# A quarter of the MLP's inner rows for chunks 0 to 8, worked out in native fp32 products while the attention runs

## The chip, the cores and the metric

The kernel runs on one core of one Trainium2 chip. The metric is the device time of one execution in microseconds (us); smaller is better. In every trace TensorE is PE (its weight loads PEld), VectorE is DVE, ScalarE is ACT, GpSimd is POOL and SyncE is SP.

## The reference

Two stages, in fp32. A recurrent attention over 768 steps for 4 batches and 8 heads of width 40, and then an MLP on its output for 3072 tokens:

```python
for t in range(S):                                  # attention: r, k, v, w, a, b are (4, 8, 768, 40)
    y[:, :, t] = np.einsum('bhd,bhde->bhe', rt, state)
    Sa = np.einsum('bhde,bhe->bhd', state, at)
    state_decay = state * wt[:, :, None, :] - np.einsum('bhd,bhe->bhde', Sa, bt)
    state = state_decay + np.einsum('bhd,bhe->bhde', vt, kt)
x = y.transpose(0, 2, 1, 3).reshape(3072, 320)
h = x @ w_in                                        # w_in is (320, 2048)
sp = np.where(h > 20.0, h, np.log1p(np.exp(np.minimum(h, 20.0))))
out = (h * np.tanh(sp)) @ w_out                     # Mish; w_out is (2048, 320)
```

## The kernel before

The 768 steps are cut into 12 chunks of 64; a chunk holds 256 tokens of the MLP. The attention has three kinds of work. `pre_a` (four times for two chunks) loads wa and bk through SP, makes running products of the decay on DVE, writes them to memory as pD, and multiplies on PE into `pa` tiles (L186, L202). `pre_inv` and `post_inv` invert a triangular matrix for two chunks, first on DVE (L214, L216), then on PE, and make the KT tiles (L258). `step` is the recurrence itself, one chunk after another: L284 into `pu`, negated by ACT into UVT (L286), transposes (L293, L304), L314 into `pq`, masked by DVE into UVQ (L316), then L334 and L339, from which DVE takes the new state and ACT the output yev, which goes to memory as yD through POOL's queue. All products of the attention are native fp32.

The MLP reads yD and pD of a chunk back (`load_x`, eight DMAs on SP), multiplies them on DVE (L565), and splits the result into a high and a low part of type fp32r (xh, xl). Each weight is split in the same way (`split`: a DMA of 512 or 640 columns into cv_d, ACT, three DVE instructions, ACT, DVE). The 2048 inner rows are worked through in four quarters q of 512. For a quarter, `mlp1` makes 32 products of 256 columns into `ph` (L583), ACT applies Mish (L585) and rounds (L588), DVE takes the low part (L589); `mlp2` makes 24 products of 320 columns into `po` (L603 to L605), three quarters later. After the fourth quarter ACT copies po out (L609) and SP stores it.

The pieces of weights are converted in stages that the program names: `early` (the first quarter of w_in: three pieces, at the start of the attention), `first` (the other three quarters: nine pieces, after the last `pre_a`), `second` (w_out pieces 0 to 2, behind the last `post_inv`) and `third` (w_out 3 to 7). The number of cv_d buffers of a stage is CVE, CVA, CVD, CVC. PSUM has eight banks: two for pu, two for pq, two for the pa of the inverse (`ps_a`), two for the pa of `pre_a` (`ps_g`); in the MLP four of them are ph and four po.

The framework sorts each engine's instructions into one list when the program is built, by priorities, by when it expects operands and buffers to be there, and by its own estimates of cost; OFF holds offsets of priority for parts of the program (positive is earlier). The engine then works through its list from front to back.

Of the kernel before, what the change touches and what calls it, by code (L numbers as in the profile page):

```python
# [7 lines left out]
F32 = mybir.dt.float32  # L8
# [8 lines left out]
NBKN = 8  # L17
NA = 2
NWA = 2
# [5 lines left out]
NGP = 2  # L25
NG = 2
NQ = 2
# [9 lines left out]

OFF = {'I': 80, 'T1': 80, 'P00': -40, 'P10': 80, 'P11': 40, 'b0': 15, 'c0': 600, 'u0': -15, 'u1': 250, 'd0': 250,
       'd1': 150, 'W': 600, 'V': 400, 'E': 150, 'I0': 600, 'I1': -15, 'I2': 15, 'I3': 150, 'I4': 80, 'p4': 15,
# [39 lines left out]
def attention(ctx, tc, I, yD, pD, nch, M):  # L79
# [336 lines left out]
NQ0 = 1  # L416
NQ1 = 4
NO1 = 3
CVW = 512
CVO = 640  # L420
CVE = 1
CVD = 1
CVA = 1
CVB = 1
CVC = 2
NX = 2
NXP = 1
NHB = 3
# [16 lines left out]
def load_f32(nc, pool, w, src):  # L445

    V, A, SP = nc.vector, nc.scalar, nc.sync
    n = w.shape[1]
    if src.dtype == F32:
        SP.dma_start(out=w, in_=src)  # L450
        return 1.0
    d = pool.tile([128, n, 2], I32, name="cv_d")
    SP.dma_start(out=d.rearrange("p a b -> p (a b)"), in_=src.bitcast(I32))
    lo, hi = d[:, :, 0], d[:, :, 1]
    m = pool.tile([128, n], I32, name="cv_m")
    w = w.bitcast(I32)


    A.mul(m.bitcast(F32), hi.bitcast(F32), 2.0 ** -111)

    V.tensor_scalar(w, m, 0xfffffff, 3, op0=ALU.bitwise_and, op1=ALU.logical_shift_left)
    V.scalar_tensor_tensor(out=w, in0=m, scalar=-0x80000000, in1=w, op0=ALU.bitwise_and, op1=ALU.bitwise_or)
    V.scalar_tensor_tensor(out=w, in0=lo, scalar=29, in1=w, op0=ALU.logical_shift_right, op1=ALU.bitwise_or)
    return 2.0 ** -8
# [14 lines left out]
class Mlp:  # L479


    def __init__(self, ctx, tc, I, yD, pD, out):
        self.ctx, self.tc, self.I, self.yD, self.pD, self.out = ctx, tc, I, yD, pD, out
        self.ih, self.il, self.oh, self.ol = [], [], [], []

# [11 lines left out]
    def w_in(self, wp, cv, qs):  # L497
        for q in qs:
            h = wp.tile([128, 3, 512], F32R, name=f"w_ih{q}")
            l = wp.tile([128, 3, 512], F32R, name=f"w_il{q}")  # L500
            self.ih.append(h)
            self.il.append(l)
            for k in range(3):
                for c in range(0, 512, CVW):
                    s = slice(c, c + CVW)
                    self.split(cv, h[:, k, s], l[:, k, s], self.I['wi'][:, (q * 3 + k) * 512 + c:(q * 3 + k) * 512 + c + CVW])

    def w_out(self, wp, cv, qs):
        for q in qs:
            h = wp.tile([128, 640], F32R, name=f"w_oh{q}")  # L510
            l = wp.tile([128, 640], F32R, name=f"w_ol{q}")
            self.oh.append(h)
            self.ol.append(l)
            for c in range(0, 640, CVO):
# [3 lines left out]
    def early_pools(self, ctx):  # L518
        if NQ0:
            self.wpe = self.pool("w2e", 1)  # L520
            self.cve = ctx.enter_context(self.tc.tile_pool(name="cve", bufs=CVE, side="right"))

    def early(self):
        if NQ0:
            self.w_in(self.wpe, self.cve, range(NQ0))

    def first(self):
        wp = self.pool("w2a", 1)
        with self.tc.tile_pool(name="cva", bufs=CVA, side="right") as cv:
            self.w_in(wp, cv, range(NQ0, NQ1))  # L530

    def second(self):
        self.ps_h = self.pool("ps_h", NH, space=PSUM)
        if NQ1 < 4:
            wp = self.wp = self.pool("w2b", 1)
            with self.tc.tile_pool(name="cvb", bufs=CVB, side="right") as cv:
                self.w_in(wp, cv, range(NQ1, 4))
        self.mpx = self.pool("mpx", 2)
        self.mpa = self.pool("mpa", 2)
        if NO1:  # L540
            wp = self.pool("w2d", 1)
            with self.tc.tile_pool(name="cvd", bufs=CVD, side="right") as cv:
                self.w_out(wp, cv, range(NO1))

# [5 lines left out]
    def run(self, nsc):  # L550
# [7 lines left out]
        def load_x(i):  # L558
            y = self.mpx.tile([128, 3, T], F32, name="xy", bufs=NXP)
            p = self.mpx.tile([128, 3, T], F32, name="xp", bufs=NXP)  # L560
            load_yp(nc, i, yD, pD, y, p, True)
# [3 lines left out]
            V.tensor_tensor(out=y, in0=y, in1=p, op=ALU.mult)  # L565
# [3 lines left out]
            return xh, xl  # L569

        def mlp1(q, xh, xl):
            g = mpa.tile([128, 4, T], F32, name="g", bufs=NHB)
# [20 lines left out]

        def mlp2(i, q, gh, gl):
            if q == 0:
                pos[i] = [ps_o.tile([128, 320], F32, name="po") for _ in range(2)]
            po = pos[i]
            for j in range(4):
                f = q * 4 + j
                for k in range(2):  # L600
                    t = slice(k * 128, k * 128 + 128)
                    oh, ol = (w[f // 2][:, f % 2 * 320:f % 2 * 320 + 320] for w in (W.oh, W.ol))
                    PE.matmul(po[k], gh[:, j, t], oh, start=(f == 0), stop=False, skip_group_check=True)  # L603
                    PE.matmul(po[k], gh[:, j, t], ol, start=False, stop=False, skip_group_check=True)  # L604
                    PE.matmul(po[k], gl[:, j, t], oh, start=False, stop=(f == 15), skip_group_check=True)  # L605
            if q == 3:
                for k in range(2):
                    o = mp.tile([128, 320], F32, name="os")
                    A.copy(o, po[k])  # L609
                    SP.dma_start(out=out[i * T + k * 128:i * T + k * 128 + 128], in_=o)  # L610
# [3 lines left out]
        for i in range(nsc):  # L614
            for q in range(4):
                wait.append((i, q) + mlp1(q, *x))
                if (i, q) == (0, 0):
                    self.third()
                if q == 1 and i + 1 < nsc:
                    nx = load_x(i + 1)  # L620
# [7 lines left out]
def build(tc, I, out, nch):  # L628
    with ExitStack() as ctx:
        dp = ctx.enter_context(tc.tile_pool(name="dp", bufs=1, space=bass.MemoryType.DRAM))  # L630
        yD = dp.tile([nch, 2, 40, 2, 512], F32, name="yD")
        pD = dp.tile([nch, 2, 40, 2, 520], F32, name="pD")
        M = Mlp(ctx, tc, I, yD, pD, out)
        with ExitStack() as actx:
# [23 lines left out]
```

## Time and profile before

| | |
|---|---|
| median of three runs | 835.8 us (835.5 to 837.83) |
| span of the profiled execution | 843.5 us |
| mean granted PE clock | 0.939 |
| PE busy | 748.6 us (89%), 7816 records |
| PEld busy | 695.6 us (82%) |
| DVE busy | 462.0 us (55%) |
| ACT busy | 429.0 us (51%) |
| POOL busy | 103.3 us (12%) |

The span is from the first to the last instruction of one execution; no other time of that execution is listed, and it lies 7.7 us above the median of the runs. PE's busy time counts a record from its start to its modelled end, so records that follow closely overlap: where the prediction needs the cost of a product, it takes the distance between starts. A native fp32 product leaves two records in the trace, an fp32r product one.

```profile
PE   2645898998989889889799899999999999999998
DVE  6789879739899658788924639221222222122110
ACT  4533647774586866566738546333333333333331
PEclk9855689899999999899959999999999999999999
```

Each digit is the busy share of a fortieth of the span (21 us) in tenths. The attention fills the first 24 of them, the MLP the rest, where PE alone is full.

### The profile page before, as it was taken

The numbers are of one execution on the slowest core, as the hardware profiler recorded it, in microseconds if no ns is written. First come the engines' busy times: TensorE is split into PE (matmuls) and PEld (weight loads), VectorE is DVE, ScalarE is ACT, GpSimd is POOL, SyncE is SP. The second block draws the span as 40 slices with busy tenths as digits, with TensorE's granted clock in tenths as the row PEclk, the third lists the DMA queues.
The fourth block names the chain that finished last, engine by engine and source line by source line (L and its number), as shares of the span: only waits on it lengthen the run. The fifth ranks groups of instructions, "written<-read, shape, count | busy, mean of one in ns | idle before, by whom it ended". The sixth has DMA issues, their size and how long they took to land.

```text
span 843.5 us, 18796 instructions
## 1 busy us (share of the span) xinstructions
PE 748.6 (89%) x7816; PEld 695.6 (82%) x7816; DVE 462.0 (55%) x975; ACT 429.0 (51%) x937; POOL 103.3 (12%) x182
## 2 busy tenths in 40 slices
PE   2645898998989889889799899999999999999998
PEld 2534697887868778778768799999999999999998
DVE  6789879739899658788924639221222222122110
ACT  4533647774586866566738546333333333333331
POOL 8100012113122023221101200000000000000000
PEclk9855689899999999899959999999999999999999
DMA  6422223323423233323425734211120111100000
GB/s 177 134 71 64 74 63 73 90 67 105 129 81 80 66 88 103 82 67 96 123 66 142 179 109 128 54 35 36 38 54 25 31 54 35 35 21 16 16 1 32
DMA packets 58212, 61.91 MB, mean 73 GB/s; under 512 B 25536, under 2 KB 48704, under 8 KB 58128
## 3 DMA queue, kind: packets, MB, share of 16 engines
q1 hardware_dynamic: 49296, 40.94, 17.6%
q0 software_dynamic: 8832, 19.79, 9.5%
q8 instruction: 61, 1.00, 0.5%
q14 instruction: 23, 0.19, 0.1%
HBM read 48.79 MB, written 11.86 MB: 72 GB/s over the span
## 4 chain that ended last, share of the span: by engine, by line
PE 62%; DVE 15%; ACT 15%; issue 5%; DMA 2%; ACTq 0%; DVEq 0%; SPq 0%
PE ph L583 21%; PE po L604 7%; PE po L605 7%; PE po L603 7%; PE pa L186 5%; PE pa L258 4%; PE pq L314 3%; PE pq L334 2%; DVE XL L216 2%; DVE tmp L214 2%; ACT ad L155 2%; PE pu L284 1%; DMA cv_d<-in_wo 1%; DVE P L147 1%; ACT bdT L250 1%
## 5 line engine op out<-in xcount | busy, mean ns | idle before, releaser
L583 PE MATMUL ph<-xh,w_ih 128*128 128x256 f32 x576 | 148.3, 283 | 0.5 <-ACT xh L566 0.5
L585 ACT ACTIVATE g<-ph 128x512 f32<-128x512 f32 x96 | 57.3, 598 | 179.3 <-PE ph L583 179.2
L589 DVE TENSOR_TENSOR gl<-g,gh 128x1024 fp32r<-128x1024 f32 x48 | 58.7, 1225 | 160.7 <-ACT gh L588 160.4
L583 PE MATMUL ph<-xh,w_il 128*128 128x256 f32 x576 | 123.6, 283 | 0.0
L186 PE MATMUL pa<-bk,ad 128*128 128x168 f32 x384 | 85.0, 373 | 42.7 <-DVE bk L170 15.0
L604 PE MATMUL po<-w_ol,gh 128*128 128x320 f32 x384 | 118.8, 310 | 0.1
L605 PE MATMUL po<-w_oh,gl 128*128 128x320 f32 x384 | 118.4, 309 | 0.0
L603 PE MATMUL po<-w_oh,gh 128*128 128x320 f32 x384 | 117.7, 309 | 0.0
L186 PEld LDWEIGHTS pa<-bk,ad 128*128 128x128 f32 x384 | 70.8, 233 | 47.8 <-issue 22.8
L583 PEld LDWEIGHTS ph<-xh,w_ih 128*128 128x128 f32 x576 | 109.3, 190 | 0.7 <-ACT xh L566 0.7
L583 PE MATMUL ph<-xl,w_ih 128*128 128x256 f32 x384 | 101.2, 285 | 0.0
L583 PEld LDWEIGHTS ph<-xh,w_il 128*128 128x128 f32 x576 | 96.3, 190 | 0.0
L583 PEld LDWEIGHTS ph<-xl,w_ih 128*128 128x128 f32 x384 | 73.1, 190 | 0.8 <-issue 0.5
L604 PEld LDWEIGHTS po<-w_ol,gh 128*128 128x128 f32 x384 | 72.1, 188 | 0.5 <-DVE w_ol L495 0.5
L605 PEld LDWEIGHTS po<-w_oh,gl 128*128 128x128 f32 x384 | 72.1, 188 | 0.1
L603 PEld LDWEIGHTS po<-w_oh,gh 128*128 128x128 f32 x384 | 71.8, 188 | 0.0
L258 PE MATMUL pa<-bdT,HA 128*104 128x128 f32 x384 | 57.0, 304 | 9.0 <-ACT bdT L251 7.3
L258 PEld LDWEIGHTS pa<-bdT,HA 128*104 128x104 f32 x384 | 49.9, 190 | 14.4 <-ACT bdT L251 9.1
L216 DVE TENSOR_TENSOR XL<-XL,tmp 128x30 f32<-128x30 f32 (+9 forms) x180 | 59.0, 328 | 2.4
L214 DVE TENSOR_TENSOR tmp<-XL 128x30 f32<-128x30 f32 (+9 forms) x180 | 58.5, 325 | 2.5
L314 PE MATMUL pq<-bdr,UVT 128*128 128x128 f32 x384 | 57.3, 294 | 2.3 <-DVE UVQ L316 1.5
L314 PEld LDWEIGHTS pq<-bdr,UVT 128*128 128x128 f32 x384 | 50.8, 205 | 4.0 <-DVE UVQ L316 1.9
(89 smaller groups left out, 1243.5 us busy)
## 6 DMA issues: line engine op xcount, KB each, us to landing
wa<-in_wa SPq DMA_DIRECT2D x48, 162.5 KB
bk<-in_bk SPq DMA_DIRECT2D x48, 160.0 KB
cv_d<-in_wi SPq DMA_DIRECT2D x12, 512.0 KB
cv_d<-in_wo SPq DMA_DIRECT2D x8, 640.0 KB
pD<-P POOLq DMA_DIRECT2D x48, 81.2 KB, 2.2
VS<-in_vN POOLq DMA_DIRECT2D x24, 160.0 KB, 3.6
UVT<-in_vD POOLq DMA_DIRECT2D x24, 160.0 KB, 3.9
bdr<-in_rD POOLq DMA_DIRECT2D x24, 160.0 KB, 4.4
```

The costliest lines, as they stand in the source:

```text
L155: A.copy(ad[q, :, :, al], a[q].rearrange("p (s k t) -> p s k t", k=2, t=32))
L186: PE.matmul(pt[:, j], ad[:, s0 + j].rearrange("p k a t -> p (k a t)"), bk[:, s0 + j], start=(j == 0), stop=True, skip_group_check=True)
L214: V.tensor_tensor(out=tv, in0=X[:, i + 1:32, i:i + 1].broadcast_to([128, 31 - i, i]), in1=X[:, i:i + 1, 0:i].broadcast_to([128, 31 - i, i] ...
L216: V.tensor_tensor(out=X[:, i + 1:32, 0:i], in0=X[:, i + 1:32, 0:i], in1=tv, op=ALU.add)
L258: PE.matmul(pk[:, j], ha[:, s0 + j], bd[:, s0 + j].rearrange("p a t -> p (a t)"), start=(j == 0), stop=True, skip_group_check=True)
L314: PE.matmul(pq[:, s], UVT[:, g * 4 + s, be * 128:be * 128 + 128], br[:, be, g * 4 + s].rearrange("p a t -> p (a t)"), start=(s == 0), stop ...
L583: PE.matmul(o, w, x, start=(j == 0 and n == 0), stop=(n == 7), skip_group_check=True)
L585: A.activation(g[:, f0:f0 + 2], ph, AF.Mish)
L589: V.tensor_tensor(out=gl, in0=g, in1=gh.bitcast(F32), op=ALU.subtract)
L603: PE.matmul(po[k], gh[:, j, t], oh, start=(f == 0), stop=False, skip_group_check=True)
L604: PE.matmul(po[k], gh[:, j, t], ol, start=False, stop=False, skip_group_check=True)
L605: PE.matmul(po[k], gl[:, j, t], oh, start=False, stop=(f == 15), skip_group_check=True)
```

## The change

For chunks 0 to 8 the first quarter of the inner rows (q = 0) leaves the MLP. A new function `fill` does it: it loads y of a finished chunk, makes 12 native fp32 products of 256 columns with an unsplit copy of the first quarter of w_in (L541), Mish into gn, eight native products of 320 columns with the first quarter of w_out (L548), in two blocks of four, and stores the two partial results in memory (`part`, L560). It is written behind step i + 1 of the attention, with a priority that is 3000 lower; the load of y and its product (L530) keep the normal one. In the MLP the chunk then has three quarters, and DVE adds the partial result, read back through SP, where ACT copied. Chunks 9 to 11 do the same first quarter natively inside the MLP (`first_quarter` in `load_x`, `second_quarter` in `mlp2`), summed in po.

Buffers: the two pa pools become one of three banks (`ps_r`), and `fill` has one bank (`ps_f`). xy, xp and gn have one buffer each, shared by fills and MLP. The weights' stages change: `early` loads eight unsplit pieces (four of w_in with 384 columns, four of w_out with 320), `first` six pieces with two buffers, `second` three of w_in and three of w_out with one buffer, `third` three.

```diff
-NA = 2
-NG = 2
+NR = 3
+NF = 9
-OFF = {'I': 80, 'T1': 80, ...
+OFF = {'F': -3000, 'I': 80, 'T1': 80, ...
...
-    ps_a = pool("ps_a", NA, ictx, "right", space=PSUM)
+    ps_a = ps_g = pool("ps_r", NR, ictx, "right", space=PSUM)
+    ps_f = pool("ps_f", 1, ictx, "right", space=PSUM)
     M.early_pools(pctx)
-    ps_g = pool("ps_g", NG, pctx, "right", space=PSUM)
...
                 step(2 * n + int(k))
+                if 0 <= 2 * n + int(k) - 1 < NF:
+                    M.fill(2 * n + int(k) - 1, ps_f)
...
-NO1 = 3
+NO1 = 5
-CVA = 1
+CVA = 2
...
+    def load_y(self, i):
+        y = self.wpe.tile([128, 3, 256], F32, name="xy")
+        p = self.wpe.tile([128, 3, 256], F32, name="xp")
+        load_yp(self.tc.nc, i, self.yD, self.pD, y, p, True)
+        self.tc.nc.vector.tensor_tensor(out=y, in0=y, in1=p, op=ALU.mult)
+        return y
+
+    def first_quarter(self, y, ps):
+        nc = self.tc.nc
+        g = self.wpe.tile([128, 4, 256], F32, name="gn")
+        for f0 in (0, 2):
+            ph = ps.tile([128, 2, 256], F32, name="ph")
+            for j in range(2):
+                f = slice((f0 + j) * 128, (f0 + j) * 128 + 128)
+                for k in range(3):
+                    nc.tensor.matmul(ph[:, j], self.ni[:, k, f], y[:, k], start=(j == 0 and k == 0), stop=(k == 2), skip_group_check=True)
+            nc.scalar.activation(g[:, f0:f0 + 2], ph, AF.Mish)
+        return g
+
+    def second_quarter(self, g, po, k, last):
+        t = slice(k * 128, k * 128 + 128)
+        for j in range(4):
+            self.tc.nc.tensor.matmul(po, g[:, j, t], self.no[:, j], start=(j == 0), stop=(last and j == 3), skip_group_check=True)
+
+    def fill(self, i, ps):
+        nc = self.tc.nc
+        y = self.load_y(i)
+        with at(self.tc, 'F'):
+            g = self.first_quarter(y, ps)
+            for k in range(2):
+                po = ps.tile([128, 2, 256], F32, name="ph").rearrange("p a b -> p (a b)")[:, 0:320]
+                self.second_quarter(g, po, k, True)
+                o = self.wpe.tile([128, 320], F32, name="part", bufs=2)
+                nc.scalar.copy(o, po)
+                nc.sync.dma_start(out=self.part[i, k], in_=o)
...
-            self.w_in(wp, cv, range(NQ0, NQ1))
+            self.w_in(wp, cv, range(1, 3))
...
+            self.w_in(wp, cv, range(3, 4))
+            self.w_out(wp, cv, range(2, NO1))
...
+            gn = self.first_quarter(y, ps_h) if i >= NF else None
...
-            if q == 0:
+            if q == 1:
                 pos[i] = [ps_o.tile([128, 320], F32, name="po") for _ in range(2)]
+                for k in range(2 if gn is not None else 0):
+                    self.second_quarter(gn, pos[i][k], k, False)
...
-                    A.copy(o, po[k])
+                    if i < NF:
+                        p = mp.tile([128, 320], F32, name="pp")
+                        SP.dma_start(out=p, in_=self.part[i, k])
+                        V.tensor_tensor(out=o, in0=po[k], in1=p, op=ALU.add)
+                    else:
+                        A.copy(o, po[k])
...
-            for q in range(4):
+            for q in range(1, 4):
```

Where the lists place this is seen on PE. A row is one instruction or several alike in a row (line, operation, tile written, tiles read, shape, count); L541 and L548 are the fills, L583 (L611 after the change) is `mlp1`. Before the change, the list of PE around the attention's last product (L339):

```order
L334 MATMUL pq<-UVQ_120,bkn 64x64
L339 MATMUL pq<-bdr_121,smd 64x2x64 x4
L583 MATMUL ph<-xl,w_ih_5096 128x256
L583 MATMUL ph<-xh,w_il_5097 128x256 x2
L583 MATMUL ph<-xh,w_ih_5096 128x256
L583 MATMUL ph<-xh,w_il_5097 128x256
```

The MLP is already in its third quarter there. The same place after the change, from the last L339 to the first L611 (the lines left out repeat the two rows above them three times):

```order
L339 MATMUL pq<-bdr_124,smd 64x2x64 x4
L548 MATMUL ph<-w_no,gn 128x320
L541 MATMUL ph<-xy,w_ni 128x256 x12
L548 MATMUL ph<-w_no,gn 128x320 x8
...
L541 MATMUL ph<-xy,w_ni 128x256 x12
L548 MATMUL ph<-w_no,gn 128x320 x8
L611 MATMUL ph<-xh,w_ih_5443 128x256 x2
```

The last product of fill 3 and the whole of fills 4 to 8 stand behind the attention, and the MLP's first product behind them. Fills 0 to 2 and the other 19 products of fill 3 are spread over the attention from step 1 on. One of the five, fill 4, with what its products wait for (DMAHW are SP's loads, Activation is ACT):

```order
L541 MATMUL ph<-xy,w_ni 128x256 [waits DMAHW7_49,Activation_49]
L541 MATMUL ph<-xy,w_ni 128x256 [waits DMAHW0_49]
L541 MATMUL ph<-xy,w_ni 128x256 [waits DMAHW2_49,DMAHW1_49]
L541 MATMUL ph<-xy,w_ni 128x256 x3
L541 MATMUL ph<-xy,w_ni 128x256 [waits Activation_49]
L541 MATMUL ph<-xy,w_ni 128x256 x5
L548 MATMUL ph<-w_no,gn 128x320 [waits Activation_49]
L548 MATMUL ph<-w_no,gn 128x320 x3
L548 MATMUL ph<-w_no,gn 128x320 [waits Activation_49]
L548 MATMUL ph<-w_no,gn 128x320 x3
```

Each of its four blocks waits for ACT to have emptied the one bank of ps_f. The last step of the attention (step 11), before the change, from its L284 on; 33 products of L583 stand between:

```order
L284 MATMUL pu<-KT,VS_117 64x64 x8
L583 MATMUL ph<-xh,w_ih_5064 128x256
...
L583 MATMUL ph<-xl,w_ih_5096 128x256
L583 MATMUL ph<-xh,w_ih_5096 128x256
L314 MATMUL pq<-bdr_121,UVT 128x128 x16
L334 MATMUL pq<-UVQ_119,bkn 64x64
```

And after it:

```order
L284 MATMUL pu<-KT,VS_120 64x64 x8
L541 MATMUL ph<-xy,w_ni 128x256 x4
L548 MATMUL ph<-w_no,gn 128x320 x4
L314 MATMUL pq<-bdr_124,UVT 128x128 x8
L548 MATMUL ph<-w_no,gn 128x320 x3
L314 MATMUL pq<-bdr_124,UVT 128x128 x8
L334 MATMUL pq<-UVQ_122,bkn 64x64
```

Products of fill 3 stand where products of L583 stood, and two of their blocks wait for ACT ahead of L314.

More of the change, by code (lines that the diff above doesn't have):

```diff
@@ L415 @@
 NH = 4
-NQ0 = 1
-NQ1 = 4
-NO1 = 3
+NO1 = 5
 CVW = 512
 CVO = 640
-CVE = 1
 CVD = 1
-CVA = 1
-CVB = 1
+CVA = 2
 CVC = 2
 NX = 2
-NXP = 1
 NHB = 3
@@ L454, in load_f32 @@
     lo, hi = d[:, :, 0], d[:, :, 1]
-    m = pool.tile([128, n], I32, name="cv_m")
+    m = hi
     w = w.bitcast(I32)
@@ L479, with __init__ @@
 class Mlp:
-    def __init__(self, ctx, tc, I, yD, pD, out):
-        self.ctx, self.tc, self.I, self.yD, self.pD, self.out = ctx, tc, I, yD, pD, out
-        self.ih, self.il, self.oh, self.ol = [], [], [], []
+    def __init__(self, ctx, tc, I, yD, pD, part, out):
+        self.ctx, self.tc, self.I, self.yD, self.pD, self.part, self.out = ctx, tc, I, yD, pD, part, out
+        self.ih, self.il, self.oh, self.ol = {}, {}, {}, {}
     def pool(self, n, b, side="right", **k):
@@ L500, in w_in @@
             l = wp.tile([128, 3, 512], F32R, name=f"w_il{q}")
-            self.ih.append(h)
-            self.il.append(l)
+            self.ih[q], self.il[q] = h, l
             for k in range(3):
@@ L511, in w_out @@
             l = wp.tile([128, 640], F32R, name=f"w_ol{q}")
-            self.oh.append(h)
-            self.ol.append(l)
+            self.oh[q], self.ol[q] = h, l
             for c in range(0, 640, CVO):
@@ L518, in early_pools @@
     def early_pools(self, ctx):
-        if NQ0:
-            self.wpe = self.pool("w2e", 1)
-            self.cve = ctx.enter_context(self.tc.tile_pool(name="cve", bufs=CVE, side="right"))
+        self.wpe = self.pool("w2e", 1)
+        self.ni = self.wpe.tile([128, 3, 512], F32, name="w_ni")
+        self.no = self.wpe.tile([128, 4, 320], F32, name="w_no")
+        self.cve = ctx.enter_context(self.tc.tile_pool(name="cve", bufs=1, side="right"))
     def early(self):
-        if NQ0:
-            self.w_in(self.wpe, self.cve, range(NQ0))
+        nc = self.tc.nc
@@ new lines, in early @@
+        for w, src in [(self.ni.rearrange("p k f -> p (k f)")[:, k:k + 384], self.I['wi'][:, k:k + 384]) for k in range(0, 1536, 384)] + \
+                [(self.no[:, k], self.I['wo'][:, k * 320:k * 320 + 320]) for k in range(4)]:
+            f = load_f32(nc, self.cve, w, src)
+            if f != 1.0:
+                nc.scalar.mul(w, w, f)
+        nc.gpsimd.memset(self.ni[64:128, 2], 0.0)
+    def load_y(self, i):
[4 more added lines that the diff above has]
+        return y
@@ L529, in first @@
         with self.tc.tile_pool(name="cva", bufs=CVA, side="right") as cv:
-            self.w_in(wp, cv, range(NQ0, NQ1))
+            self.w_in(wp, cv, range(1, 3))
     def second(self):
         self.ps_h = self.pool("ps_h", NH, space=PSUM)
[L534 to L537, printed above, removed]
         self.mpx = self.pool("mpx", 2)
         self.mpa = self.pool("mpa", 2)
[L540 to L543, printed above, removed]
+        wp = self.pool("w2d", 1)
+        with self.tc.tile_pool(name="cvd", bufs=CVD, side="right") as cv:
+            self.w_in(wp, cv, range(3, 4))
+            self.w_out(wp, cv, range(2, NO1))
     def third(self):
@@ L558, in load_x @@
         def load_x(i):
-            y = self.mpx.tile([128, 3, T], F32, name="xy", bufs=NXP)
-            p = self.mpx.tile([128, 3, T], F32, name="xp", bufs=NXP)
-            load_yp(nc, i, yD, pD, y, p, True)
+            y = self.load_y(i)
             xh = self.mpx.tile([128, 3, T], F32R, name="xh", bufs=NX)
             xl = self.mpx.tile([128, 2, T], F32R, name="xl", bufs=NX)
-            V.tensor_tensor(out=y, in0=y, in1=p, op=ALU.mult)
+            gn = self.first_quarter(y, ps_h) if i >= NF else None
             A.copy(xh, y)
@@ L568, in load_x, with mlp1 @@
             V.tensor_tensor(out=xh[64:128, 2], in0=y[64:128, 2], in1=xh[64:128, 2].bitcast(F32), op=ALU.subtract)
-            return xh, xl
-        def mlp1(q, xh, xl):
+            return gn, xh, xl
+        def mlp1(q, gn, xh, xl):
             g = mpa.tile([128, 4, T], F32, name="g", bufs=NHB)
@@ L602, in mlp2 @@
                     oh, ol = (w[f // 2][:, f % 2 * 320:f % 2 * 320 + 320] for w in (W.oh, W.ol))
-                    PE.matmul(po[k], gh[:, j, t], oh, start=(f == 0), stop=False, skip_group_check=True)
+                    PE.matmul(po[k], gh[:, j, t], oh, start=(f == 4 and i < NF), stop=False, skip_group_check=True)
                     PE.matmul(po[k], gh[:, j, t], ol, start=False, stop=False, skip_group_check=True)
@@ L614, in run @@
         for i in range(nsc):
-            for q in range(4):
-                wait.append((i, q) + mlp1(q, *x))
-                if (i, q) == (0, 0):
+            for q in range(1, 4):
+                wait.append((i, q, x[0]) + mlp1(q, *x))
+                if (i, q) == (0, 1):
                     self.third()
-                if q == 1 and i + 1 < nsc:
+                if q == 2 and i + 1 < nsc:
                     nx = load_x(i + 1)
@@ L632, in build @@
         pD = dp.tile([nch, 2, 40, 2, 520], F32, name="pD")
-        M = Mlp(ctx, tc, I, yD, pD, out)
+        part = dp.tile([nch, 2, 128, 320], F32, name="part")
+        M = Mlp(ctx, tc, I, yD, pD, part, out)
         with ExitStack() as actx:
```

5 lines of the change are left out of this document (3 added, 2 removed).

## Prediction, on record before the result was known

> **What bounds the kernel now.** I read the stretches first, cut where the trace changes character (start, busy time of PE and its weight loads, DVE, ACT, POOL, then the granted clock, DMA share and GB/s), then the chain that ended last, then PE's own rows.
>
> ```profile
> 130.00:456.00 326.00, 287.77 (x4085) 250.12 (x4078) 243.59 (x602) 218.97 (x556) 65.78 (x116) 0.94 0.33 87
> 456.00:496.40 40.40, 37.12 (x475) 33.71 (x475) 21.42 (x34) 20.26 (x38) 5.53 (x8) 1.00 0.63 151
> 496.40:843.50 347.10, 343.36 (x2601) 342.50 (x2597) 91.87 (x97) 127.66 (x184) 1.00 (x2) 1.00 0.15 42
> PE 62%; DVE 15%; ACT 15%; issue 5%; DMA 2%; ACTq 0%; DVEq 0%; SPq 0%
> L339 PE MATMUL pq<-bdr,smd x352: 272/273/476, 166.5 to 496.3; 128*64 128x128 f32 x176
> ```
>
> The attention's last matmul (L339) starts at 496.3. Behind it lie 347.1 us in which PE is busy for 343.4: the MLP is bound by PE alone. Before it no engine is. PE has 62% of the chain, 523 us; less the 343 behind 496.4, some 180 of the attention's 496 us, or 36%. The rest is DVE, ACT and waits.
>
> The MLP's pace, from the chain in order of time (start, us, engine, tile, line):
>
> ```profile
> 542.39 3.83 PE ph L583 x32
> ...
> 821.95 3.83 PE ph L583 x32
> ```
>
> Between these two lie 38 quarters (32 products of w_in, 24 of w_out): 279.56 / 38 = 7.357 us each. One product of 256 columns takes 3.83 / 32 = 0.120 us, one of 320 columns (7.357 - 3.83) / 24 = 0.147. All 48 quarters are 353.1 us. Part of them already runs inside the attention (L583 alone, from 455 on):
>
> ```profile
> 455.00:496.40 41.40, 12.44 (x91) 11.23 (x91) 1.00 0.62 150
> ```
>
> 91 x 0.120 = 10.9 us. So the 347.1 us are 353.1 - 10.9 = 342.2 of products and 4.9 of first waits and of the last store.
>
> **What a native quarter costs.** The attention's products are native fp32 already:
>
> ```profile
> 488.81 3.95 PE L314 MATMUL pq<-bdr,UVT 128*128 128x128 f32 x32
> L314 PE MATMUL pq<-bdr,UVT x384: 272/275/582, 116.0 to 492.5; 128*128 128x128 f32 x192
> ```
>
> The program holds 16 such products in this place and the trace 32 records, two for each product. A record of 128 columns takes (3.95 - 0.275) / 31 = 0.1185 us, as long as an fp32r product of 256 columns: a native record costs twice its columns, a native product four times. On the line through 0.120 at 256 and 0.147 at 320, a record of 256 native columns costs 0.229 and one of 320 costs 0.283, so a product 0.457 and 0.567. A quarter of a chunk has 12 and 8 of them: 5.49 + 4.53 = 10.0 us, where three fp32r products each cost 7.36. Scaled from 0.237 for 128 columns alone it would be 10.4, the upper end. So PE's whole work grows by 12 x (10.0 - 7.36) = 32 us; the change can only pay with what it hides.
>
> The Trainium skill's page "FP8 and Floating Point Precision" (TensorE Precision Notes) counts four passes for true fp32, and "TensorE: Matmul & The Clock Gate" (Back-to-back issue gap) gives N / 2.4 + 2.5 ns for a pass. By these a native quarter is an estimated 9.6 us, and the sum below would be 3 us less. The same rule makes an fp32r quarter 6.75 where the trace has 7.36, so I keep the rows.
>
> **Where the fills stand.** PE's order decides: fills 0 to 2, and 19 of the 20 products of fill 3, stand before the attention's last L339. Fills 4 to 8 stand behind it, one after the other, and the first L611 stands behind them all. So five of nine are not hidden by the attention, and nothing of the MLP runs beside them on PE.
>
> A fill behind the attention is PE's 10.0 us plus four hand-overs, since ps_f has one bank: Mish, Mish, copy, copy, each between two blocks of products. The nearest such wait is L284, then UVT on ACT, then L293:
>
> ```profile
> 456.78 1.09 PE L293 MATMUL pu<-cst,UVT 128*128 128x128 f32 x8 [0.86 <-ACT UVT L286]
> L286 ACT ACTIVATE UVT<-pu 128x512 f32<-128x512 f32 x24 | 14.4, 600 | 14.4 <-PE pu L284 14.4
> L585 ACT ACTIVATE g<-ph 128x512 f32<-128x512 f32 x96 | 57.3, 598 | 179.3 <-PE ph L583 179.2
> L609 ACT COPY os<-po 128x320 f32<-128x320 f32 x24 | 10.2, 427 | 29.0 <-PE po L605 28.9
> PE pu L293 <- ACT UVT L286: 7.2, 8, 1.9
> ```
>
> PE stands idle 0.86 for 0.600 on ACT. Add 0.157 of the last record's own tail (0.275 - 0.1185): 1.02 for a Mish (0.598), and with 0.427 in place of 0.600, 0.85 for a copy. A fill is 10.0 + 2 x 1.02 + 2 x 0.85 = 13.8 us. Lower end: ACT's own time alone, 12.1. Upper end: 10.4 and 1.9 at each (the longest of the eight waits of L293 for UVT, last row), 18.
>
> The next y has one buffer, free when the twelfth product is done; 7.2 us of the fill then remain. A load in the MLP:
>
> ```profile
> 740.11 0.83 SPq L472 DMA_DIRECT2D xy<-yD  x2
> 744.09 0.96 DVE L565 TENSOR_TENSOR xy<-xy,xp 128x768 f32<-128x768 f32 x1 [2.80 <-DMA xy<-yD]
> ```
>
> Issue to landing 4.0, the product 0.96: 5.0, hidden with 2 us to spare. If the DVE or SP queue is held up longer, that excess is paid five times. The part stores (SP) and the additions of partials (DVE, 24 in place of 24 ACT copies) lie beside PE's 22 us a chunk: nothing. Were their loads late, the two spare banks of ps_o would cover one chunk. In chunks 9 to 11 gn has one buffer, so that Mish of chunk 10 waits for the second products of chunk 9 and holds two of the four ph banks meanwhile: 0 to 3 us, taken at nothing, since the other two banks go on.
>
> Behind the attention then: 1.4 (last product and copy of fill 3) + 5 x 13.8 = 68.8 + 36 x 7.357 = 264.9 + 3 x 10.0 = 30.1 for chunks 9 to 11 + 4.9 = 370.1, against 347.1: **+23.0**, if the attention ends where it did.
>
> **Where the attention ends.** Fill 3's 9.5 us replace the 10.9 us of L583: nothing. Fills 0 to 2 put 30 us on PE between 130 and 456, where 38 are shown idle. A product costs when the chain is on PE: 36% of 30 = **+10.8** (ends 0 and 30; waits of PE for a Mish that is queued behind attention copies on ACT are in this spread). A fill's eight loads and two stores go through SP, ahead of wa and bk of later chunks, and a y that comes late holds DVE, which multiplies it in order. Now wa is never late:
>
> ```profile
> L145 DVE TENSOR_REDUCE w<-wa 128x8 f32<-128x256 f32 x24 | 9.9, 410 | 0.5 <-PE pa L166 0.4
> ```
>
> DVE idles 0.5 us in all before its first use of wa, none of it for a DMA; that lead covers SP's part, at nothing. Were it gone, each of three fills could cost a load's 4.0 us, 12 in all: it counts to the upper end.
>
> Weights:
>
> ```profile
> 391.58 5.02 DMA cv_d<-in_wi
> ...
> 399.95 3.47 DMA cv_d<-in_wi
> ...
> 462.89 3.83 DMA cv_d<-in_wo
> ...
> 471.60 4.50 DMA cv_d<-in_wo
> ```
>
> In the chain DVE and ACT wait for converted weights four times. The first stage now converts six pieces with two buffers instead of nine with one: the 8.5 us of in_wi can go. The second has six with one buffer where it had three: the 8.3 us of in_wo can come once more. Together **-0.2** (ends -17 and +12). The early conversion has eight pieces where it had three:
>
> ```profile
> 60.00:100.00 40.00, 26.50 (x142) 22.10 (x144) 36.47 (x92) 17.19 (x54) 3.04 (x6) 0.63 0.24 72
> L462 DVE SCALAR_TENSOR_TENSOR cv_w<-cv_m,cv_w 128x512 int32<-128x512 int32 x12 | 8.2, 686 | 0.2
> L463 DVE SCALAR_TENSOR_TENSOR cv_w<-cv_d,cv_w 128x512 int32<-128x512 int32 x12 | 8.3, 688 | 0.2
> L495 DVE SCALAR_TENSOR_TENSOR w_il<-cv_w,w_ih 128x512 fp32r<-128x512 f32 x12 | 8.2, 687 | 5.2 <-ACT w_ih L494 5.2
> L461 DVE TENSOR_SCALAR cv_w<-cv_m 128x512 int32<-128x512 int32 x12 | 5.1, 428 | 10.4 <-ACT cv_m L459 10.2
> PE pa L202 <- ACT bkn L203: 5.4, 5, 1.2
> ```
>
> DVE: 1.80 per 512 columns for four of 384 and four of 320, 9.9, against 3 x 2.49 = 7.5, in a stretch where it is busy 36.5 of 40: **+2** (0 to 5). Three PSUM banks for what had two and two: PE waits little for the emptying of pa today (last row: 5.4 us in five times behind 130); **+2** (0 to 10). A clock kept up by more work on PE:
>
> ```profile
> 434.00:455.00 21.00, 20.07 (x260) 15.87 (x258) 7.45 (x17) 14.01 (x31) 2.77 (x4) 0.76 0.34 92
> ```
>
> 0.76 of full speed over 21 us is 5 us lost, 36% of it on the chain: **-2** (0 to -7). Together +12.6.
>
> **The sum**: 843.5 + 23.0 + 12.6 = 879 for the profiled execution. It stood 7.7 over the median of the runs, 835.8, so I predict 835.8 + 35.6 = **871**.
>
> **Rivals.** (A) The attention absorbs its fills and ends up to 11 us earlier: the waits of 8.5 and 8.3 both vanish and the half-clock stretches fill up. For it: 38 us of idle PE. Against: the conversions behind 456 double in number. 835.8 + 23 - 11 to 835.8 + 23 - 3 is 848 to 856; chance 0.14. The Trainium skill's page "TensorE: Matmul & The Clock Gate" (Part 1) says that an idle window of about 3.4 us halves the clock. By that rule the fills would lift all of the 0.94 above to 1.00, an estimate of 7 us on the chain, and this case would follow; the stretch at 0.76 shows PE busy 20.07 of 21, so the trace speaks only in part for it.
> (B) PE's order stalls the attention: fills wait there for ACT, with attention products behind them, and pa has fewer banks. At the upper ends (30 + 10 + 12) the attention ends 40 us and more later: 895 to 910; chance 0.11.
> (C) Faster: the conversions set the attention's end, not PE. Their loads stand in the chain from 391 to 476; two buffers in the first stage would save about six loads of 3.5 us, 21, and with nothing else lost and fills of 12.1 the end is 835.8 + 23 - 8.5 - 21 = 829. It decides from an attention that ends by 474 on. Against it: three of the pieces only move behind 456. Chance 0.04 for all below 838.
> (D) All nine fills hidden, as the words of the change have it: excluded by PE's order.
> The forecast's own case, 856 to 890, has 0.71.
>
> **How the numbers follow.** The range 848 to 900 leaves out C, half of B and a little of A: less than 2 in 10. Within 0.3% (833.3 to 838.3, about what three runs from 835.5 to 837.8 can tell from no change) only an attention 21 to 25 us shorter would come: 0.02. Faster 0.03, slower 0.95.
>
> **What would show it.** L541 and L548 of fills 4 to 8 in one stretch behind the last L339, some 69 us long, PE idle four times a fill for Mish and part; a period of 22 us a chunk behind it up to chunk 8; the last L339 near 509. A stretch of 60 or 90, or a last L339 before 490 or after 530, would make the forecast wrong; a native record of 256 columns far from 0.229 would fell the price of a fill.

## The result, and the profile after

The changed kernel takes 893.2 us (median of four runs, 886.65 to 895.18) against 836.2 for the kernel before in the same session: a ratio of 1.067 (95% interval 1.062 to 1.071). It is slower, as forecast, by 57.0 us where the forecast had 35.2 (871 less 835.8) and its range ended at 900. The two traced executions differ by 49.9 (spans 893.4 and 843.5). The span after belongs to the execution that took 895.2 us, 2 us above the median; the one before lies 7 us above its median, and some 9 if that span, too, is 1.8 us shorter than its time. So 7 us of the 22 that the forecast missed are not in the traces; 14.3 are (49.9 against 35.6). Where the 7 lie no trace shows. The stretch behind the attention hardly varies (347.1 us here, 347.5 in run 2 and 347.3 in run 12 below, which have the same MLP), so most likely they lie in the attention too.

The stretches of the profile after, in the columns of the prediction's first fence (start and end, length, busy time of PE, its weight loads, DVE, ACT, POOL, then granted clock, DMA share, GB/s):

```profile
0.00:119.00 119.00, 50.12 (x598) 45.97 (x599) 75.85 (x173) 50.80 (x123) 27.53 (x49) 0.74 0.34 93
529.50:893.40 363.90, 347.16 (x2340) 324.27 (x2338) 88.48 (x106) 109.63 (x160) 1.00 (x2) 1.00 0.24 65
```

The chain that ended last, by engine, and the row of L339 (count, shortest, median and longest in ns, first and last start):

```profile
PE 60%; DVE 15%; ACT 14%; DMA 6%; issue 5%; SPq 0%; ACTq 0%; DVEq 0%
```

```profile
L339 PE MATMUL pq<-bdr,smd x352: 272/273/323, 148.8 to 529.3; 128*64 128x128 f32 x176
```

The last L339 starts at 529.3, where it started at 496.3: the attention ends 33.0 later, and the forecast had +12.6. The chain moved little (DMA has 6% where it had 2%). Behind the attention lie 363.9 us where 347.1 lay: +16.8, and the forecast had +23.0.

PE's order of time behind the attention (start, us, what; in brackets the idle time before and what ended it):

```profile
530.81 2.86 PE L541 MATMUL ph<-xy,w_ni 128*128 128x256 f32 x12 [0.52 <-ACT part L559]
534.42 2.86 PE L541 MATMUL ph<-xy,w_ni 128*128 128x256 f32 x12 [0.75 <-ACT gn L542]
537.96 2.42 PE L548 MATMUL ph<-w_no,gn 128*128 128x320 f32 x8 [0.69 <-ACT gn L542]
540.90 2.42 PE L548 MATMUL ph<-w_no,gn 128*128 128x320 f32 x8 [0.52 <-ACT part L559]
```

This is one fill behind the attention, as the forecast described it: four blocks, each behind a wait for ACT. The next fill's first row starts 13.11 later, and the five end at 596.3, 65.5 us in all (forecast 68.8).

Where the 33 us went shows at the other end of the attention. First before, then after: PE's products of `pre_a` (L186) and of the first inverse (L232), then the start (L209) and the end (L218) of the second inverse on DVE, and the last state of step 2 (L346).

```profile
60.82 4.78 PE L186 MATMUL pa<-bk,ad 128*128 128x168 f32 x16 [10.60 <-ACT ad L155]
...
92.47 4.21 PE L186 MATMUL pa<-bk,ad 128*128 128x168 f32 x16 [1.07 <-ACT rw L168]
...
99.24 1.82 PE L232 MATMUL pa<-TT,GP 32*32 32x32 f32 x64 [0.24 <-DVE TT L218]
101.82 2.10 DVE L209 STREAM_TRANSPOSE XL<-GP 128x1024 f32<-128x1024 f32 x1
149.93 1.98 DVE L218 STREAM_TRANSPOSE TT<-XL 128x1024 f32<-128x1024 f32 x1
...
207.98 0.48 DVE L346 TENSOR_TENSOR ST<-stn,R 128x320 f32<-128x320 f32 x1
```

```profile
88.40 1.92 PE L232 MATMUL pa<-TT,GP 32*32 32x32 f32 x64 [39.78 <-DVE TT L218]
...
120.20 2.45 PE L186 MATMUL pa<-bk,ad 128*128 128x168 f32 x16
...
141.72 2.14 DVE L209 STREAM_TRANSPOSE XL<-GP 128x1024 f32<-128x1024 f32 x1
197.46 1.90 DVE L218 STREAM_TRANSPOSE TT<-XL 128x1024 f32<-128x1024 f32 x1
...
238.16 0.48 DVE L346 TENSOR_TENSOR ST<-stn,R 128x320 f32<-128x320 f32 x1
```

Before, PE works through the four `pre_a` of chunks 2 and 3 while DVE does the first inverse. After, PE stands idle for 39.78 us there, and those `pre_a` come behind the whole first inverse, from 120.2 on. The second inverse needs them, so it starts 40 us later, and step 2 needs the second inverse. Step 2 ends at 208.0 before and at 238.2 after: 30 us are lost by then, with 16 of the 180 products of the nine fills done. From step to step the lag then moves between 23 and 41 us, and it is 33 at the last L339.

The list of PE had shown it, at a place where the forecast did not look. After the change (`...` stands for rows that are left out):

```
L202 MATMUL pa<-cst,bk_102 128x128 x8
L232 MATMUL pa<-TT,GP 32x32 x32
...
L258 MATMUL pa<-bdT_106,HA 104x128 x8
...
L258 MATMUL pa<-bdT_107,HA 104x128 x6
L186 MATMUL pa<-bk_101,ad_103 128x168 x8
```

### The profile page after: what moved, and what is told of

The parts are those of the page before. It is cut to its first block, busy times and chain, and to the rows that moved or that the text cites. A ratio compares the mean times of both kernels' runs of the same rounds, so it can differ in the third digit from the quotient of the medians.

```text
span 893.4 us, 18624 instructions
## 1 busy us (share of the span) xinstructions
PE 760.2 (85%) x7624; PEld 681.7 (76%) x7624; DVE 465.6 (52%) x994; ACT 417.3 (47%) x931; POOL 105.1 (12%) x183
## 4 chain that ended last, share of the span: by engine, by line
PE 60%; DVE 15%; ACT 14%; DMA 6%; issue 5%; SPq 0%; ACTq 0%; DVEq 0%
PE ph L611 15%; PE ph L541 6%; PE pa L186 6%; PE po L635 5%; PE po L634 5%; PE po L633 5%; PE pa L258 3%; PE ph L548 3%; DMA cv_d<-in_wi 3%; DMA cv_d<-in_wo 2%; ACT ad L155 2%; PE pq L314 2%; DVE tmp L214 2%; DVE XL L216 2%; PE pq L334 2%
## 5 line engine op out<-in xcount | busy, mean ns | idle before, releaser
L611 PE MATMUL ph<-xh,w_ih 128*128 128x256 f32 x432 | 111.2, 283 | 0.6 <-ACT part L559 0.6
L186 PE MATMUL pa<-bk,ad 128*128 128x168 f32 x384 | 78.6, 359 | 31.1 <-DVE bk L170 15.0
L186 PEld LDWEIGHTS pa<-bk,ad 128*128 128x128 f32 x384 | 68.0, 225 | 36.2 <-issue 30.1
L611 PE MATMUL ph<-xh,w_il 128*128 128x256 f32 x432 | 92.5, 283 | 0.0
L633 PE MATMUL po<-w_oh,gh 128*128 128x320 f32 x288 | 90.1, 313 | 0.0
L634 PE MATMUL po<-w_ol,gh 128*128 128x320 f32 x288 | 88.9, 309 | 0.0
L635 PE MATMUL po<-w_oh,gl 128*128 128x320 f32 x288 | 88.9, 309 | 0.0
L611 PEld LDWEIGHTS ph<-xh,w_ih 128*128 128x128 f32 x432 | 82.1, 190 | 1.1 <-ACT part L559 1.1
L541 PE MATMUL ph<-xy,w_ni 128*128 128x256 f32 x288 | 72.6, 395 | 10.1 <-ACT gn L542 7.4
L611 PE MATMUL ph<-xl,w_ih 128*128 128x256 f32 x288 | 75.3, 283 | 0.0
L611 PEld LDWEIGHTS ph<-xh,w_il 128*128 128x128 f32 x432 | 72.2, 190 | 0.0
L541 PEld LDWEIGHTS ph<-xy,w_ni 128*128 128x128 f32 x288 | 52.6, 193 | 22.8 <-ACT gn L542 10.2
L316 DVE TENSOR_TENSOR UVQ<-pq,cst 128x512 f32<-128x512 f32 x48 | 32.4, 683 | 46.5 <-PE pq L314 46.4
L611 PEld LDWEIGHTS ph<-xl,w_ih 128*128 128x128 f32 x288 | 54.9, 190 | 0.0
L530 DVE TENSOR_TENSOR xy<-xy,xp 128x768 f32<-128x768 f32 x21 | 20.1, 957 | 66.7 <-DMA xy<-yD 60.9
```

Of the source, the lines that this page charges most:

```text
L186: PE.matmul(pt[:, j], ad[:, s0 + j].rearrange("p k a t -> p (k a t)"), bk[:, s0 + j], start=(j == 0), stop=True, skip_group_check=True)
L316: V.tensor_tensor(out=UVQ[be][:, g * 8:g * 8 + 8, 0:64], in0=pq.rearrange("p s (a t) -> p (s a) t", a=2), in1=maskQ.unsqueeze(1).broadcast ...
L541: nc.tensor.matmul(ph[:, j], self.ni[:, k, f], y[:, k], start=(j == 0 and k == 0), stop=(k == 2), skip_group_check=True)
L611: PE.matmul(o, w, x, start=(j == 0 and n == 0), stop=(n == 7), skip_group_check=True)
L633: PE.matmul(po[k], gh[:, j, t], oh, start=(f == 4 and i < NF), stop=False, skip_group_check=True)
```

## The experiments

All ratios are to the kernel before, run in the same session. There are three sessions, in which the kernel before took 841.6 us (runs 1 to 4), 837.0 (5 to 8) and 840.1 (9 to 12); across sessions, ratios are compared and not times. Where the attention ends is read from one traced execution of each kernel, and executions of one kernel differ by up to 1.5% (run 8), so a few us between two traces tell nothing by themselves. The theory formed from the traces, called S: the one pool of three banks, shared by `pre_a` and the inverse, hands its banks out in the order in which the program is written. `pre_a` of chunks 2 and 3 is written behind the first inverse, so it waits for all of that inverse's tiles; in a pool of its own it did not. The rivals: F, the fills' own products; W, the weights' conversions; Y, the loads of y that hold DVE.

**1. The shared pool alone**, in the kernel before:

```diff
-    ps_a = pool("ps_a", NA, ictx, "right", space=PSUM)
+    ps_a = ps_g = pool("ps_r", 3, ictx, "right", space=PSUM)
-    ps_g = pool("ps_g", NG, pctx, "right", space=PSUM)
+    pool("ps_f", 1, ictx, "right", space=PSUM)
```

> The kernel before with one edit: the two pa pools of two banks become one of three, as in the changed kernel; the fourth bank stays empty. Theory S (shared pool): a pool hands out its banks in the order in which the program is written, and the four pre_a of chunks 2 and 3 are written behind the inverse of chunks 0 and 1, so with one pool their products must wait for all of that inverse's pa tiles. Then the second inverse begins (L209) near 140 instead of 101.8, ends (L218) near 195 instead of 150, and the attention's last L339 comes 20 to 30 us later: 855 to 866 us in all. Theory F (the fills' own products cost the 33 us): merging costs the +2 of the forecast, last L339 at 496 to 500, 836 to 840 us. Theory W (the weights' conversions cost it): the same as F here.

Measured: 886.5 us, ratio 1.053 (1.048 to 1.057). The second inverse, from DVE's order of time:

```profile
140.74 2.17 DVE L209 STREAM_TRANSPOSE XL<-GP 128x1024 f32<-128x1024 f32 x1
198.72 1.88 DVE L218 STREAM_TRANSPOSE TT<-XL 128x1024 f32<-128x1024 f32 x1
```

No fill, no other conversion, and the same late inverse, at the same times within 1.3 us. The last L339 is at 538.9. The size was missed: 45 us where 20 to 30 were expected.

**2. The same, with the program's order mended**: the four `pre_a` are written ahead of the first inverse.

```diff
     pa(0)
-    inv(0)
     for u in range(4):
         with at(tc, 'P%d%d' % (u // 2, u % 2)):
             pre_a(2 + u // 2, u % 2)
+    inv(0)
```

> The kernel before with one pa pool of three banks, as in the run before, and the four pre_a of chunks 2 and 3 written ahead of the first inverse instead of behind it. No work is added or left out. Theory S: the four pre_a get their banks first, the second inverse begins near 102 again, and most of what the shared pool cost is back: 834 to 845 us. If three banks are too few in themselves, and not their order: no better than the run before, 855 to 866. Theories F and W: both runs stand within 4 us of the kernel before.

Measured: 847.5 us, ratio 1.007 (1.0035 to 1.010).

```profile
100.76 2.08 DVE L209 STREAM_TRANSPOSE XL<-GP 128x1024 f32<-128x1024 f32 x1
141.11 2.00 DVE L218 STREAM_TRANSPOSE TT<-XL 128x1024 f32<-128x1024 f32 x1
```

The inverse is back at 100.8. Of 5.3% the order was 4.6; what is left, 0.7% or 6 us, is the price of three banks in place of four together with the new order (no run has that order with four banks), inside the forecast's 0 to 10 for the banks.

**3. The changed kernel without fills** (`NF = 0`).

> The changed kernel with NF = 0: no fill, all twelve chunks do the first quarter natively in the MLP. The shared pool and the new stages of the weights stay. Theory S: the last L339 stays late, at 515 to 530, since no fill was needed to make it so. Theory F: it returns to 496 to 505. Theory W: it stays at 515 to 530 too, but the second inverse begins near 102 and the time is lost behind 380. Behind the last L339 come 12 x (22.07 + 9.5) = 379 us and some 5 of first waits, less what of the MLP runs in the attention: 895 to 915 us by S and W, 875 to 890 by F.

Measured: 904.3 us, ratio 1.073; last L339 at 539.3, L209 of the second inverse at 144.8. The attention is late without any fill, and from the start on: F and W fall as the cause of the 33 us.

**4. The changed kernel with the order mended**, the edit of run 2.

> The changed kernel with one edit: the four pre_a of chunks 2 and 3 are written ahead of the first inverse instead of behind it. Theory S: the second inverse begins near 105 instead of 141.7 and the attention's last L339 moves from 529 to 500 to 510, the stretch behind it stays at 364: 864 to 876 us, which is about the forecast. Theory F or W: 888 to 896 us, unchanged.

Measured: 872.0 us, ratio 1.035 (1.028 to 1.041): 3.2 points come back, 27 us.

```profile
111.08 2.09 DVE L209 STREAM_TRANSPOSE XL<-GP 128x1024 f32<-128x1024 f32 x1
152.04 2.02 DVE L218 STREAM_TRANSPOSE TT<-XL 128x1024 f32<-128x1024 f32 x1
```

```profile
L339 PE MATMUL pq<-bdr,smd x352: 271/273/324, 170.9 to 492.2; 128*64 128x128 f32 x176
```

The last L339 comes 37 us earlier than in the changed kernel. Some 27 of them show in the time, since the stretch behind it is 375.6 us where 364 were expected:

```profile
492.20:867.80 375.60, 355.36 (x2374) 329.74 (x2369) 90.10 (x108) 111.67 (x165) 1.00 (x2) 1.00 0.24 65
```

Now 4 of the 20 products of fill 3 stand ahead of the last L339, where 19 stood, and the other 16 are paid behind it. Beside the kernel before, the attention ends 4 us earlier in these two traces; by the medians, less the stretches behind the attention, it ends about 2 us later (872.0 - 375.6 against 841.6 - 347.1), so the two are not told apart. S is shown, from both sides: the shared pool alone makes the inverse late (run 1), and the order alone brings it back, without fills (run 2) and with them.

**5. Run 4, with fills 4 to 8 in the four ph banks** in place of the one bank of ps_f:

```diff
-                if 0 <= 2 * n + int(k) - 1 < NF:
+                if 0 <= 2 * n + int(k) - 1 < 4:
                     M.fill(2 * n + int(k) - 1, ps_f)
...
                 M.second()
+            for i in range(4, NF):
+                M.fill(i, M.ps_h)
```

> The run before (the changed kernel with the pre_a of chunks 2 and 3 written ahead of the first inverse, 872.0 us) with one edit: fills 4 to 8 take the four ph banks of the MLP instead of the one bank of ps_f. Theory H (hand-overs): a fill behind the attention took 13.11 us where its products take 9.5; the rest is PE waiting for ACT to empty the one bank, four times. With four banks two or three of these go, and the distance from fill to fill falls to 10.0 to 11.2; five fills save 10 to 16 us: 856 to 862. Rival Y: the single xy buffer and its load of 5 us set the distance, and it stays at 13: 869 to 875.

Measured: 856.7 us, ratio 1.022 (1.014 to 1.030): 1.25 points or some 10 us less than run 4, the small end of what theory H had. The two intervals just overlap; the rows show the cause.

```profile
542.40 5.45 PE L543 MATMUL ph<-xy,w_ni 128*128 128x256 f32 x24 [0.60 <-DVE xy L532]
547.68 4.47 PE L550 MATMUL ph<-w_no,gn 128*128 128x320 f32 x16
552.68 5.45 PE L543 MATMUL ph<-xy,w_ni 128*128 128x256 f32 x24 [0.53 <-DVE xy L532]
```

The waits for ACT are gone from these rows and 10.3 us lie from fill to fill; what is left is a wait of 0.5 for y (the first two of the five still lie 12.1 apart, with 2.36 for y). The hand-overs are shown. The Trainium skill's page "Perfetto Trace Analysis" (Optimizing Tensor Performance, Matmuls) says that independent groups of matmuls should rotate through different PSUM banks, so that one is emptied while the next is filled; these rows agree, with 13.11 on one bank and 10.3 on four.

**6. Run 4 with only fills 0 to 3** (`NF = 4`).

> The same base (872.0 us) with NF = 4: only fills 0 to 3 exist, chunks 4 to 11 do their first quarter natively inside the MLP, where the products took 9.5 us a chunk (chunks 9 to 11 of the changed kernel) and the four ph banks hide the hand-overs. Theory H: five fills at 13.1 become five native quarters at 9.5 to 10: 852 to 858, and the attention's end stays within 5 us. Rival: the native quarter in the MLP is no cheaper, since gn has one buffer and Mish of the next chunk waits for it: 868 to 875.

Measured: 850.9 us, ratio 1.018 (1.013 to 1.023): 1.7 points or some 14 us less than run 4, the small end of the 14 to 20 that H had. In the chain, a native quarter inside the MLP is 5.18 + 4.31 = 9.5 (0.216 and 0.269 a record):

```profile
662.08 5.18 PE ph L541 x24
...
681.98 4.31 PE po L548 x16
```

A fill that is not hidden is dearer behind the attention (13.1) than inside the MLP (9.5), and either is dearer than the fp32r quarter that it replaces (7.36).

**7. Run 4 with the load of y at the fill's low priority.**

```diff
-        y = self.load_y(i)
         with at(self.tc, 'F'):
+            y = self.load_y(i)
             g = self.first_quarter(y, ps)
```

> The same base (872.0 us) with the load of y and its product at the low priority of the fill's products, so that DVE meets L530 later in its list. In the changed kernel DVE stood 60.9 us in 13 waits for xy. Theory S: these waits stand where DVE has slack or behind the attention; no more than 4 us: 868 to 876. Theory Y: a held DVE holds the inverse and the masks behind it, and 10 us or more come back: 855 to 864, with the last L339 before 485.

Measured: 878.2 us, ratio 1.051 (1.046 to 1.057), last L339 at 508.8: later, not earlier. Y falls. Against run 4's ratio it is 1.7 points or 14 us slower, which is outside S too (4 us at most). The last state of step 7 comes at 387.1 in this run and at 387.0 in run 4, that of step 8 at 430.5 and at 419.1; what delays step 8 is open. DVE's waits for xy in run 4 (sum in us, times, longest), in the whole span and then up to 490:

```profile
DVE xy L530 <- DMA xy<-yD: 81.5, 14, 13.0
...
DVE xy L530 <- DMA xy<-yD: 2.3, 2, 1.5
```

All but 2.3 us of them stand behind the attention.

**8. Run 4 with three fills, and fp32r quarters for the first rows of chunks 3 to 11** (split by ACT and DVE from the unsplit copies, during the MLP; the third block of y has 64 rows in the fills):

```diff
-NF = 9
+NF = 3
...
+        for h, l, w in [(self.ih[0][:, k], self.il[0][:, k], self.ni[:, k]) for k in range(3)] + \
+                [(self.oh[q], self.ol[q], no[:, q * 640:q * 640 + 640]) for q in range(2)]:
+            A.copy(h, w)
+            V.tensor_tensor(out=l, in0=w, in1=h.bitcast(F32), op=ALU.subtract)
...
-            for q in range(1, 4):
+            for q in range(1 if i < NF else 0, 4):
```

> The same base with NF = 3, so that all fills stand inside the attention, and chunks 3 to 11 do their first quarter in split fp32r products like the other quarters; the split copies of the first quarter of the weights are made from the native ones by ACT and DVE during the MLP, and the native fills use 64 rows for the third block of y. If fills inside the attention cost it little once the order is mended (its last L339 stood at 492.2 with fills 0 to 2), the MLP keeps 45 quarters of 7.357, less some 5 us of products that stand in the attention, plus 4.9: 492 + 331 = 823 us of span, 820 to 830. If fills cost 36% of their PE time (theory F), the attention ends near 503 and the time is 833 to 842, about the kernel before. Rival: the five split copies hold ACT and DVE beside the MLP and PE waits: 845 or more.

Measured: 829.6 us, ratio 0.991 (0.9865 to 0.995): 0.9% less than the kernel before, a small difference whose interval leaves out 1, and 7% less than the changed kernel.

**9. Run 8 with its fills left out** (the first quarter of chunks 0 to 2 is not computed).

> The kernel with three fills (829.6 us) with its fills left out: nothing works out the first quarter of chunks 0 to 2, and their partials are not added. This prices the forecast's +10.8 for fills 0 to 2 inside the attention. In the lists 125 products of the MLP (15 us) now stand ahead of the last L339 where 44 (5 us) stood. If the fills were nearly free (theory S): the last L339 stays at 496 to 503, and the time falls by the 10 us of products that moved in front: 817 to 824. If each product of a fill cost 36% of its time (theory F): the last L339 at 488 to 493, and 806 to 814.

Measured: 829.0 us, ratio 0.985 (0.980 to 0.9905), last L339 at 501.8. From 130 to the last L339, in this run and in run 8:

```profile
130.00:501.80 371.80, 323.43 (x4593) 290.08 (x4591) 271.36 (x641) 240.95 (x595) 73.38 (x127) 0.94 0.37 100
```

```profile
130.00:502.20 372.20, 344.13 (x4669) 296.95 (x4669) 273.82 (x645) 243.42 (x605) 74.71 (x128) 0.96 0.39 102
```

And the fills' products in run 8 (busy time, mean ns, idle time of PE ahead of them):

```profile
L541 PE MATMUL ph<-xy,w_ni 128*128 128x256 f32 (+1 forms) x72 | 24.9, 452 | 0.0
```

PE never waits ahead of a fill (L548 has 0.0 too). Run 9 has 125 products of the MLP in this stretch and run 8 has 44 and the three fills: PE is busy 20.7 us longer with the fills, and the attention ends 0.4 later. So three fills are hidden, in place of some 10 us of the MLP's products. F falls here too. The time, scaled to run 8's session, is 824.5, just above what S gave; the products that moved in front left the stretch behind only 4 us shorter, 325.7 for 329.7. The medians agree: the two ratios lie 0.6 points or 5 us apart, and 4 of these are that stretch.

**10 and 11. Run 8 with four and with six fills, at a priority 300 lower instead of 3000**, which puts all of them ahead of the last L339.

> The kernel with three fills, with NF = 4 and the fills' priority lowered by 300 instead of 3000. In the lists all four fills and 121 products of the MLP then stand ahead of the last L339 (before: three and 44). PE has 9.5 + 9.3 us more to do in the attention and 16.6 less behind it. If the attention's idle PE takes them (theory S): 814 to 823. If they push the attention's end by as much: 829 to 833.

> The same with NF = 6: six fills (57 us of PE) and 107 products of the MLP stand ahead of the last L339; PE has 36 us more to do in the attention than with three fills, and 29.7 less behind it. Between steps 2 and 5 of the changed kernel PE was already busy 96% of the time (62.4 of 65 us), so at least a part must push the end: if half of it is hidden, 815 to 825; if nothing is, 834 to 840.

Measured: 845.5 us (ratio 1.006, 1.003 to 1.010) and 842.1 (1.000, 0.997 to 1.004). Scaled to run 8's session these are 842 and 837: the first is worse than either expectation, the second is what was expected if nothing is hidden. Run 10, and then run 11:

```profile
130.00:528.40 398.40, 366.80 (x4789) 312.54 (x4787) 279.02 (x649) 248.66 (x614) 74.62 (x128) 0.97 0.38 100
```

```profile
130.00:537.40 407.40, 380.61 (x4845) 317.79 (x4843) 278.39 (x649) 251.27 (x619) 74.56 (x128) 0.99 0.39 103
```

From run 8 to run 10 PE gains 22.7 us of work and the attention 26.2 of length; to run 11, 36.5 and 35.2. From run 9 to run 8 it was 20.7 and 0.4. PE is busy 87% of this stretch in run 9, 92% in runs 8 and 10, 93% in run 11. Read by these shares, the room ends at about 92%, and from there a microsecond of products costs a microsecond. That a full PE is the cause is argued, not shown: the priority of the fills was changed together with their number, no run has three fills at the new priority, and a fill that stands earlier in the list can also hold up the attention's own products.

**12. The weights' stages alone**, in the kernel before (`NQ1 = 3`, `CVA = 2`).

> The kernel before with only the stages of the weights changed as in the change: the first converts six pieces with two buffers instead of nine with one, the fourth quarter of w_in moves into the second stage, which then has six pieces with one buffer. The forecast's term: -0.2, so 834 to 840. Theory W (the conversions set the attention's end): 8 to 21 us less, 815 to 829. The other way (the six pieces in the second stage hold the end): 843 to 850.

Measured: 842.7 us, ratio 1.000 (0.996 to 1.004), last L339 at 495.0. Together the shifts cost nothing, as the forecast had them; W, which is the forecast's rival C, falls.

## Why the prediction was right, and where it was off

The direction and the mechanism behind the attention were right: four fills (all but one product) ahead of the last L339, five behind it in a row. The mechanism that made the attention late was not in it. That 893 us still fell inside the range was in part luck: the range was wide, 893 lies above the forecast's own case (856 to 890), and a stretch behind the attention that came out 6 us cheaper took back part of the 20 us by which the attention's end was missed. The last L339, which the forecast had near 509 and not after 530, came at 529.3. By its own steps:

- *The native record*: forecast 0.229 and 0.283. Measured from the rows above: (2.86 - 0.379) / 11 = 0.226 and (2.42 - 0.432) / 7 = 0.284 (0.379 and 0.432 are one record's own time). The price of the products held. In rows without a wait between them it is a little less, 0.216 and 0.269 (run 6).
- *A fill at 13.8*: 13.11. Products 10.0, hand-overs 0.52 to 0.75 where L284's row had led to 0.86. Five fills 65.5 for 68.8.
- *Chunks 9 to 11 at 10.0*: 9.5 each. *The MLP's 36 quarters at 7.357*: the same, 22.07 a chunk. *Partials at nothing*: right.
- The stretch behind the attention: +16.8 for +23.0; the fills (3.3) and chunks 9 to 11 (1.6) are 4.9 of the difference.
- *The attention's end, +12.6*: this step failed; it was +33.0. The term at fault is *three PSUM banks, +2 (0 to 10)*. It priced the number of banks, by how long PE waits for pa to be emptied. Run 2, with the order mended, leaves 6 us for it. What it did not see is that two users of one pool are tied to the program's order. Rival B named the place ("pa has fewer banks") and, at +40, the size, but gave it to the fills' waits.
- *Fills 0 to 2, +10.8*: too high. Runs 8 and 9 show 0.4 for three fills, in place of 10 us of the MLP's products, once the order is mended.
- *Weights, -0.2*: right (run 12). *Early conversion, +2*: not seen alone; the first inverse starts at 49.7 for 49.9. *Loads of y at nothing*: right by run 4, whose waits lie behind the attention.
- *Clock, -2*: not seen as a gain. In the changed kernel the granted clock is 0.87 from 119 to 238, where the order holds PE up, and 0.97 from there to 530; before the change it is 0.96 from 130 to 208 and 0.95 from there to 497. The kernel before, from 130 to its last L339, and run 4:

```profile
130.00:496.40 366.40, 324.90 (x4560) 283.83 (x4553) 265.02 (x636) 239.23 (x593) 71.31 (x124) 0.95 0.37 94
```

```profile
130.00:492.20 362.20, 330.81 (x4676) 288.33 (x4675) 273.06 (x649) 244.87 (x609) 75.49 (x129) 1.00 0.38 102
```

With the order mended the clock is full where it was 0.95, in these two traces; run 8 has 0.96 and run 9, without fills, 0.94. So the first half of rival A, the stretches at half clock that fill up, is seen. That the attention ends earlier for it is not shown (run 4).

What stays open: why the shared pool alone (run 1, last L339 at 538.9) ends the attention later than the changed kernel does with its fills (529.3). In run 1, 100 products of the MLP (12 us) stand ahead of that L339 and in the changed kernel none; and the granted clock, from 130 to the last L339, is 0.89 in run 1 and 0.94 in the changed kernel. Either would go that way, and no run separates them.

The whole in ratios to the kernel before: 1.067 as changed, 1.035 with the order mended, 1.018 without the late fills, 0.991 with fp32r quarters in place of the native ones in the MLP. Against run 2 (1.007), which has the one pool and the mended order but no fills and the old stages of weights, the last of these is 1.6% less.

## What to carry to other kernels

Merging two pools of banks is a change of order, not only of number: the banks go round in the order in which the code is written, and a producer written late waits for all earlier users, however early it is needed. After such an edit, look in the engine's list for work that changed places far from where the new code stands. Work moved into another stage's idle time can be free, as three fills were here, but more of it was not (runs 10 and 11), and what does not fit should go back to its cheaper form, as in run 8.

## What the runs showed of the hardware

The granted clock of PE around the idle stretch of the changed kernel (same columns as above):

```profile
60.00:70.00 10.00, 0.00 (x0) 0.00 (x0) 9.62 (x24) 1.49 (x3) 0.52 (x1) 0.50 0.45 116
92.00:96.00 4.00, 2.76 (x68) 2.65 (x69) 0.00 (x0) 1.75 (x5) 0.00 (x0) 0.50 0.01 4
100.00:104.00 4.00, 3.52 (x95) 3.20 (x94) 0.00 (x0) 2.86 (x6) 0.00 (x0) 1.00 0.02 4
```

It is half while PE idles (first row), still half in the second row, up to 7.6 us after work resumes at 88.4, and full in the third, from 11.6 us after it. The Trainium skill's page "TensorE: Matmul & The Clock Gate" (Part 1) has about 3.4 us of sustained activity as enough to release it; here it took more than 7.6 us, with PE busy 69% of the time in the second row, so this case has no sustained activity to test the figure by.

The spread between executions of one kernel goes with the clock: the ten of run 8 go from 821.5 us at a mean granted clock of 0.964 to 833.7 at 0.942. Which of the two brings about the other is not shown. A single trace can lie 1% off its kernel's median, as the one of the kernel before did.
